# Retention in 64-position chunks with values stacked on state, and all matmuls in program order

## The chip, the cores and the metric

The kernel runs on one core of a Trainium2 chip. A core has a tensor engine (PE), which multiplies a stationary block of weights (loaded by PEld) with a moving block and writes the result to PSUM; a vector engine (DVE), a scalar engine (ACT) and GpSimd (POOL), which work on SBUF (DVE and ACT on PSUM too); and a queue (SP) that issues the DMA transfers between HBM and SBUF. Engines run side by side, each through its own queue in order, and wait for each other by semaphores. The metric is the device time of one execution in microseconds, lower is better.

## The reference, cut to what matters

Two stages. First retention, a linear attention with a decay per head (gamma), over 4 batches, 8 heads, 768 positions and head size 64. Then a gated MLP in which the second half of the hidden layer is normalised and mixed over positions by `w_spatial`.

```python
gamma = 1.0 - 2.0 ** (-5.0 - np.arange(H))
for t in range(S):                                   # S = 768
    state = gamma * state + einsum('bhd,bhe->bhde', k[:, :, t], v[:, :, t])
    y[:, :, t] = scale * einsum('bhd,bhde->bhe', q[:, :, t], state)
x = y.transpose(0, 2, 1, 3).reshape(B, S, 512)
h = np.maximum(x @ w_in, 0.0)                        # 512 -> 1024
u, v = h[..., :512], h[..., 512:]
v_n = (v - mean(v)) / sqrt(var(v) + 1e-6)
v_s = einsum('ts,bsd->btd', w_spatial, v_n) + b_spatial[None, :, None]
out = (u * v_s) @ w_out
```

## The kernel before, in words

**Retention** works chunk by chunk, 128 positions each: 6 chunks a batch, 24 in all, counted by `g`. For one chunk `ret_out` forms the output x of all 8 heads in one PSUM tile: a product of masked scores p and values, plus, from the second chunk of a batch on, a product of the state and the queries. `score` forms the scores of the next chunk, `ret_update` the state after this one. `run(g)` calls the three in this order. All these products have float32 operands, except that from chunk `WHOLE` = 9 on the scores are made from operands that `stack` has split in two float32r parts (`scores_split`). DVE masks the scores of the early chunks (POOL those of the split ones), scales x by the decay of its position into `xf` (L279), and ACT and POOL split `xf` into the float32r parts `xh` and `xl` of the MLP. POOL scales each chunk's values as soon as they are loaded (L211).

**The MLP** takes all its products as three float32r products of high and low parts (`split3`, and L414 in `mlp_out`). `mlp_v` is a block of 128 positions of the second half of the hidden layer (V), `mlp_norm` its normalisation (N). A unit of the gate (I) is the first half of the hidden layer (`mlp_u`, tile u), the spatial product (`mlp_spatial`, tile sp) and the last product (`mlp_out`, tile o) of the unit before it; a batch has 8 units, and O7 closes it. PSUM has three pools: `ps_r` with three buffers for everything in retention, `ps_m` with two for v, u and sp, `ps_o` with three for o.

**The weights** of the MLP come as doubles in 12 blocks. L loads a block into `raw` (three buffers), C splits it (`split_double`): ACT and DVE pick the bits apart (L146 to L152, tiles `da` and `df`), DVE or POOL form the low part. W loads and splits a block of the spatial weights (tile `wst`).

**The order** of the parts is written as four strings of words: START (retention of batch 0 and of the first chunks of batch 1, half of the weights, V and N of batch 0), FIRST (the gate of batch 0, the other weights, the rest of retention and V, N of batch 1), REST (the gate of a batch with retention, V and N of the next), LAST (the last gate). Q loads queries and keys, T keys and values, R runs retention of a chunk. The strings give a scheduler its priorities: loads are held to the program's order on SP, all else, matmuls too, may be moved within an engine's queue by the scheduler's own estimate of times.

Of the kernel before, what the change touches and what calls it, by code (L numbers as in the profile page):

```python
# [9 lines left out]
F32 = mybir.dt.float32  # L10
# [12 lines left out]
WHOLE = 9  # L23
# [7 lines left out]
START = (  # L31
# [3 lines left out]
)  # L35
FIRST = (
    "C7 L10 I0 L11 W01 W11 W21 C8 I1 W31 C9 I2 W51 T12 C10 W41 R9 T11 I3 C11 I4 Q11 R10 "
    "Q12 I5 I6 Q13 R11 V0 I7 V1 N0 V3 V2 N1 N2 T13 N3 V5 V4 N4 N5 O7"
)
REST = (  # L40
    "R0 Q2 T2 R1 I0 I1 Q3 T3 I2 R2 Q4 T5 I3 I4 R3 T4 Q5 I5 R4 Q6 T6 I6 Q7 T7 V0 I7 R5 V1 "
# [5 lines left out]
# Order in which the blocks of the weights in double precision are split, and how many of the  # L47
# residues are formed on the vector engine.
# [7 lines left out]
def tile_retention_gmlp(  # L56
    ctx: ExitStack,
    tc: tile.TileContext,
    qk: bass.AP,
    qT: bass.AP,  # L60
    kT: bass.AP,
    kv: bass.AP,
# [8 lines left out]
    cdecay: bass.AP,  # L71
# [5 lines left out]
    NG = kv.shape[0]  # L77
    NC = NG // B
    H, D = kv.shape[3], kv.shape[4]
    NP = H // 2  # L80
# [16 lines left out]
    mask_t = wpool.tile([P, P], F32, name="mask_t")  # L97
    vd_t = wpool.tile([P, H], F32, name="vd_t")
    qd_t = wpool.tile([P, NP, P], F32, name="qd_t")
    cd_t = wpool.tile([P, NP], F32, name="cd_t")  # L100
# [11 lines left out]
    wout_l = wpool.tile([P, KT, DM], F32R, name="wout_l")  # L112

# [25 lines left out]
    def split_double(i):  # L139
# [3 lines left out]
        a = mpool.tile([P, DM], F32, tag="stage", name=f"da{i}")  # L143
# [19 lines left out]
    query = {}  # L163
    keys = {}
    kvs = {}
    stacked = {}
    scores = {}
    state = {}
    xhalf = {}

    def load_query(g):
        if g >= NG:
            return
        if g < WHOLE:
            t = rpool.tile([P, 2, NP, P], F32, tag="qk", name=f"qk{g}", bufs=3)
            load(t, qk[g])
            query[g] = [t[ROWS[h % 2], 0, h // 2] for h in range(H)]
            keys[g] = t[:, 1]
        else:
            kt = rpool.tile([P, NP, P], F32, tag="qk", name=f"k{g}", bufs=3)  # L180
            qt = rpool.tile([P, H, P], F32, tag="qk", name=f"q{g}", bufs=3)
            load(kt, kT[g - WHOLE])
            load(qt, qT[g - WHOLE])
            query[g] = [qt[ROWS[h % 2], h] for h in range(H)]
            keys[g] = kt
            stack(g, kt, qt)

    def load_value(g):
        if g >= NG:
            return  # L190
        kvs[g] = rpool.tile([P, 2, H, D], F32, tag="kv", name=f"kv{g}")
        load(kvs[g], kv[g])
        scale_v(g)

    def stack(g, kt, qt):
        k2 = mpool.tile([P, H, P], F32R, tag="raw", name=f"k2_{g}", bufs=3)
        q2 = [
            mpool.tile([P, NP, 2, P], F32R, tag="raw", name=f"q2_{g}_{i}", bufs=3)
            for i in range(2)
        ]  # L200
        for r in range(2):
            nc.scalar.copy(k2[ROWS[r], r::2], kt[ROWS[r]])
            residue(nc.vector, k2[ROWS[1 - r], r::2], kt[ROWS[r]], k2[ROWS[r], r::2])
        for i in range(2):
            qi = qt[:, NP * i : NP * i + NP]
            nc.scalar.copy(q2[i][:, :, 0], qi)  # L206
            residue(nc.gpsimd, q2[i][:, :, 1], qi, q2[i][:, :, 0])
        stacked[g] = (k2, q2)

    def scale_v(g):  # L210
        nc.gpsimd.tensor_tensor(  # L211
            kvs[g][:, 1], kvs[g][:, 1], vd_t[:, :].unsqueeze(2).broadcast_to([P, H, D]), ALU.mult
        )

    def scores_split(g):
        k2, q2 = stacked.pop(g)
        ps = []
        for i in range(2):
            p = rpool.tile([P, NP, P], F32, tag="p", name=f"p{g}_{i}", bufs=3)
            for u in range(2):  # L220
                t = ps_r.tile([P, 2, 2, P], F32, tag="ret", name=f"s{g}_{i}_{u}")
                for w in range(2):
# [317 lines left out]
```

## Time and profile before

| | |
|---|---|
| time, median of 3 runs (lowest to highest) | 451.26 us (450.74 to 451.58) |
| span of the profiled execution | 445.8 us |
| granted PE clock, mean | 0.981 |
| busy: PE / PEld / DVE / ACT / POOL | 429.1 / 352.0 / 234.2 / 159.8 / 217.6 us |
| DMA | 45.23 MB, mean 101 GB/s |

The span is what the profile records of one execution, from its first to its last instruction; the median of the runs is 5.5 us above it. Busy times of PE are those of pipelined matmuls, whose ends are modelled, so that records overlap and what a block costs is read from the start of one block to the start of the next. L numbers are lines of the kernel. A float32 matmul leaves two records in the profile, a float32r matmul one.

### The profile page before, as it was taken

How to read it: one execution, taken by the hardware profiler on the slowest of the kernel's cores; microseconds unless marked ns; L12 is line 12 of the kernel's file. 1: busy time of each engine (PE TensorE's matmuls, PEld its weight loads, DVE VectorE, ACT ScalarE, POOL GpSimd, SP SyncE). 2: the span in 40 equal slices, each digit the busy share in tenths (PEclk: the TensorE clock that was granted, in tenths of full speed). 3: DMA queues.
4: the chain of work that ended last, by engine and by line, in shares of the span. 5: the costliest groups of instructions: out<-in, count | busy, mean ns of one | idle time of the engine just before them, and what ended most of it. 6: DMA issues, size and time to landing. Idle time of an engine off the chain costs nothing.

```text
span 445.8 us, 7214 instructions
## 1 busy us (share of the span) xinstructions
PE 429.1 (96%) x2834; PEld 352.0 (79%) x2834; DVE 234.2 (53%) x397; ACT 159.8 (36%) x319; POOL 217.6 (49%) x228
## 2 busy tenths in 40 slices
PE   4998989989999999999999999999999999999995
PEld 2665657777899877887988877888879778999994
DVE  2899989883863556661423556652413534422122
ACT  2324234543434344641433433652423312411211
POOL 1457874695673627473724747365534522211110
PEclk8899999996999999999999999999999999999999
DMA  7846456434125320530213330342313000100102
GB/s 259 312 129 217 130 192 216 147 132 131 43 101 190 93 73 0 209 123 1 96 71 130 109 118 0 102 160 71 96 71 119 1 0 2 71 1 0 72 0 71
DMA packets 16881, 45.23 MB, mean 101 GB/s; under 512 B 2128, under 2 KB 4048, under 8 KB 16848
## 3 DMA queue, kind: packets, MB, share of 16 engines
q1 hardware_dynamic: 16848, 44.77, 29.7%
q8 instruction: 22, 0.36, 0.3%
q14 instruction: 11, 0.09, 0.1%
HBM read 38.48 MB, written 6.29 MB: 100 GB/s over the span
## 4 chain that ended last, share of the span: by engine, by line
PE 77%; DVE 10%; POOL 5%; issue 3%; DMA 3%; SPq 1%; ACT 0%; ACTq 0%; POOLq 0%; DVEq 0%
PE sp L316 22%; PE o L414 14%; PE u L316 14%; PE v L316 11%; PE x L261 6%; PE x L264 5%; PE s L224 3%; PE u L289 2%; DMA kv<-in_kv_dram 1%; DVE p L248 1%; DVE df L149 1%; DMA k<-in_kT_dram 1%; DVE da L151 1%; DVE da L147 1%; DVE da L150 1%
## 5 line engine op out<-in xcount | busy, mean ns | idle before, releaser
L118 POOL TENSOR_TENSOR gl<-t,gh 128x384 fp32r<-128x384 f32 x31 | 32.0, 1032 | 76.2 <-ACT gh L400 72.5
L316 PE MATMUL sp<-wsp_h,vnh 128*128 128x384 f32 x192 | 65.4, 341 | 0.0
L316 PE MATMUL sp<-wsp_l,vnh 128*128 128x384 f32 x192 | 65.0, 339 | 0.0
L316 PE MATMUL sp<-wsp_h,vnl 128*128 128x384 f32 x192 | 64.3, 335 | 0.0
L398 DVE TENSOR_TENSOR t<-sp,bsp_t 128x384 f32<-128x384 f32 (+1 forms) x34 | 17.9, 532 | 76.7 <-PE sp L316 74.3
L261 PE MATMUL x<-p,kv 128*64 128x128 f32 x384 | 45.0, 306 | 6.4 <-POOL kv L211 4.4
L118 POOL TENSOR_TENSOR xl<-xf,xh 128x512 fp32r<-128x512 f32 x24 | 35.0, 1460 | 25.5 <-ACT xh L280 23.3
L118 POOL TENSOR_TENSOR q<-q,q 128x512 fp32r<-128x512 f32 x30 | 41.1, 1380 | 11.9 <-ACT q L206 11.9
L316 PE MATMUL u<-xh,winu_h 128*128 128x384 f32 x128 | 43.9, 343 | 0.0
L261 PEld LDWEIGHTS x<-p,kv 128*64 128x64 f32 x384 | 22.0, 140 | 27.4 <-issue 19.1
L316 PE MATMUL u<-xh,winu_l 128*128 128x384 f32 x128 | 43.5, 340 | 0.0
L316 PE MATMUL u<-xl,winu_h 128*128 128x384 f32 x128 | 43.1, 337 | 0.0
L400 ACT CAST gh<-t 128x384 fp32r<-128x384 f32 (+1 forms) x34 | 16.6, 494 | 68.9 <-DVE t L399 67.8
L316 PE MATMUL v<-winv_h,xh 128*128 128x512 f32 x96 | 39.3, 411 | 0.0
L316 PE MATMUL v<-winv_h,xl 128*128 128x512 f32 x96 | 39.0, 406 | 0.0
L227 DVE TENSOR_TENSOR p<-s,lo 128x256 f32<-128x256 f32 x60 | 23.8, 419 | 28.5 <-ACT lo L226 28.3
L316 PE MATMUL v<-winv_l,xh 128*128 128x512 f32 x96 | 38.7, 404 | 0.0
L211 POOL TENSOR_TENSOR kv<-kv,vd_t 128x512 f32<-128x512 f32 x24 | 26.9, 1120 | 24.0 <-DMA kv<-in_kv_dram 17.9
L228 POOL TENSOR_SCALAR_AFFINE_SELECT p<-p 128x512 f32<-128x512 f32 x30 | 24.2, 808 | 28.8 <-DVE p L227 28.6
L414 PE MATMUL o<-wout_l,gh 128*128 128x512 f32 x96 | 37.5, 394 | 0.0
L316 PEld LDWEIGHTS sp<-wsp_h,vnh 128*128 128x128 f32 x192 | 36.0, 188 | 1.7 <-issue 0.7
L226 ACT COPY lo<-s 128x256 f32<-128x256 f32 x60 | 21.0, 374 | 45.6 <-PE s L224 40.3
(73 smaller groups left out, 878.6 us busy)
## 6 DMA issues: line engine op xcount, KB each, us to landing
kv<-in_kv_dram SPq DMA_DIRECT2D x24, 512.0 KB, 3.5
q<-in_qT_dram SPq DMA_DIRECT2D x15, 512.0 KB, 3.4
out_dram<-ot SPq DMA_DIRECT2D x23, 256.0 KB, 2.0
qk<-in_qk_dram SPq DMA_DIRECT2D x9, 512.0 KB, 5.4
k<-in_kT_dram SPq DMA_DIRECT2D x15, 256.0 KB, 3.6
wst<-in_w_sp_dram SPq DMA_DIRECT2D x12, 192.0 KB, 3.6
raw<-in_w_inv_dram SPq DMA_DIRECT2D x4, 512.0 KB, 6.6
raw<-in_w_inu_dram SPq DMA_DIRECT2D x4, 512.0 KB, 3.8
```

Of the source, the lines that this page charges most:

```text
L118: eng.tensor_tensor(out, whole, high.bitcast(F32), ALU.subtract)
L211: nc.gpsimd.tensor_tensor(kvs[g][:, 1], kvs[g][:, 1], vd_t[:, :].unsqueeze(2).broadcast_to([P, H, D]), ALU.mult)
L224: nc.tensor.matmul(t[:, w], k2[:, NP * i + h], q2[i][:, h], start=True, stop=True)
L226: nc.scalar.copy(low, t[:, :, 1])
L227: nc.vector.tensor_tensor(p[:, 2 * u : 2 * u + 2], t[:, :, 0], low, ALU.add)
L228: nc.gpsimd.affine_select(out=p, in_=p, pattern=[[0, NP], [1, P]], compare_op=ALU.is_ge, fill=0.0, base=0, channel_multiplier=-1,)
L261: nc.tensor.matmul(t[ROWS[r], hp], kvs[g][:, 1, h], ps[h], start=True, stop=(c == 0))
L264: nc.tensor.matmul(t[ROWS[r], hp], state[g][ROWS[r], hp], query[g][2 * hp + r], start=False, stop=True,)
L316: nc.tensor.matmul(ps, l, r, start=(i == 0), stop=(i == 3 * n - 1))
L398: nc.vector.tensor_tensor(t[:, c], pp[:, c], bsp_t[:, tc_], ALU.add)
L400: nc.scalar.copy(gh[:, c], t[:, c])
L414: nc.tensor.matmul(o, l[:, col], r[:, j], start=(j == 0 and n == 0), stop=(j == NJ - 1 and n == 2))
```

## The change

A chunk still has 128 positions, but is worked as two halves of 64 (index `i`). For each pair of heads `hp` and each head `r` of the pair, 64 masked scores and 64 rows of queries lie on top of each other in one tile `pq` of 128 partitions, and 64 values and the 64 rows of the state on top of each other in a tile `vs`. The output of a half is then one product of all 128 rows, without an accumulation. The decay is folded into values and outputs relative to the middle of the batch's sequence, so that the state needs no factor: `ret_update` forms k times v of each half, and the state for the next half is that plus the state before, written by DVE (ACT for the first half of a batch) straight into the rows of `vs`. Scores are float32 for all chunks; the split ones, `stack`, `scale_v` and the third constant are gone. The scores' mask is 64 wide, applied by DVE in four instructions a chunk.

Loads per chunk: two transfers for the queries and one for the keys (Q), two for the values, one for the keys in natural order and one for the table of output decays of this chunk (T); seven where there were two or three. `run` calls update, scores, output in this order. `split_double` takes its tile `da` from the ring of `xf` (two buffers). Every matmul is issued by `mm`, which holds it to the program's order on PE. In the strings, some of the R words of START stand later, and a few T words moved.

```diff
-    "Q0 v m L0 q T0 c Q1 L1 T1 L2 Z R0 Q2 L3 T2 Q3 C0 C1 L4 R1 T3 L5 C2 C3 L6 R2 Q4 T4 V0 "
-    "R3 C4 Q5 T5 V1 N0 L7 R4 V3 W10 Q6 T6 V2 W00 R5 Q7 T7 N1 N2 C5 L8 W40 W20 B W30 R6 Q8 "
-    "T8 V4 N3 R7 Q9 W50 T9 V5 N4 N5 C6 L9 R8 Q10 T10"
+    "Q0 v m L0 T0 Q1 L1 T1 L2 Z R0 Q2 L3 T2 Q3 C0 C1 L4 R1 T3 L5 C2 C3 L6 Q4 T4 R2 V0 "
+    "C4 Q5 T5 R3 V1 N0 L7 R4 V3 W10 Q6 T6 V2 W00 R5 Q7 T7 N1 N2 C5 L8 W40 W20 B W30 Q8 "
+    "T8 R6 V4 N3 Q9 W50 T9 R7 V5 N4 N5 C6 L9 Q10 T10 R8"
...
+    "C7 L10 I0 L11 W01 W11 W21 C8 I1 W31 C9 I2 W51 C10 W41 R9 T11 I3 C11 I4 Q11 R10 "
+    "T12 Q12 I5 I6 Q13 R11 V0 I7 V1 N0 V3 V2 N1 N2 T13 N3 V5 V4 N4 N5 O7"
...
+    def mm(*args, **flags):
+        tc.keep_in_program_order(nc.tensor.matmul(*args, **flags))
...
-        a = mpool.tile([P, DM], F32, tag="stage", name=f"da{i}")
+        a = rpool.tile([P, DM], F32, tag="xf", name=f"da{i}")
...
     def load_query(g):
...
+        m = rpool.tile([P, 2, 2, NP, C], F32, tag="pq", name=f"pq{g}", bufs=3)
+        kt = rpool.tile([P, 2, NP, C], F32, tag="kt", name=f"kt{g}", bufs=2)
+        for r in range(2):
+            load(m[ROWS[1 - r], r], q_in[g, ROWS[1 - r]])
+        load(kt, kT[g])
...
     def load_value(g):
...
+        w = rpool.tile([P, 2, 2, NP, D], F32, tag="vs", name=f"vs{g}", bufs=3)
+        kn = rpool.tile([P, 2, NP, D], F32, tag="kn", name=f"kn{g}", bufs=2)
         for r in range(2):
+            load(w[ROWS[r], r], v_in[g, ROWS[r]])
+        load(kn, k_in[g])
+        qd = rpool.tile([P, NP, P], F32, tag="qd", name=f"qd{g}", bufs=2)
+        load(qd, qdecay[g % NC])
+        values[g], naturals[g], decays[g] = w, kn, qd
+        for r in range(2):
+            vd = vd_t[ROWS[r], g % NC].unsqueeze(3).broadcast_to([D, 2, NP, D])
+            nc.gpsimd.tensor_tensor(w[ROWS[r], r], w[ROWS[r], r], vd, ALU.mult)
+
+    def score(g):
...
+        ts = [ps_r.tile([P, NP, P], F32, tag="ret", name=f"s{g}_{i}") for i in range(2)]
+        for hp in range(NP):
+            for i in range(2):
+                for r in range(2):
+                    col = r if i == 0 else 1 - r
+                    mm(ts[i][ROWS[col], hp, :C], kt[ROWS[1 - r], i, hp],
+                       m[ROWS[1 - r], r, i, hp], start=True, stop=True)
         for i in range(2):
+            for r in range(2):
+                col = ROWS[r if i == 0 else 1 - r]
+                mk = mask_t[col].unsqueeze(1).broadcast_to([C, NP, C])
+                nc.vector.tensor_tensor(m[ROWS[r], r, i], ts[i][col, :, :C], mk, ALU.mult)
+
+    def ret_update(g):
...
+        n = 1 if last else 2
+        ts = [ps_r.tile([P, NP, P], F32, tag="ret", name=f"u{g}_{i}") for i in range(n)]
+        for hp in range(NP):
+            for i in range(n):
+                for r in range(2):
+                    col = 1 - r if i == 0 else r
+                    mm(ts[i][ROWS[col], hp, :D], kn[ROWS[r], i, hp],
+                       w[ROWS[r], r, i, hp], start=True, stop=True)
+        for i in range(n):
+            for r in range(2):
+                u = ts[i][ROWS[1 - r if i == 0 else r], :, :D]
+                dst = w[ROWS[1 - r], r, 1] if i == 0 else values[g + 1][ROWS[1 - r], r, 0]
+                if g % NC == 0 and i == 0:
+                    nc.scalar.copy(dst, u)
+                else:
+                    nc.vector.tensor_tensor(dst, u, w[ROWS[1 - r], r, i], ALU.add)
 
     def ret_out(g):
...
+        t = ps_r.tile([P, NP, 2, C], F32, tag="ret", name=f"x{g}")
+        for i in range(2):
+            for hp in range(NP):
                 for r in range(2):
+                    rows = ROWS[r] if c == 0 and i == 0 else slice(0, P)
+                    mm(t[ROWS[r], hp, i], w[rows, r, i, hp], m[rows, r, i, hp],
+                       start=True, stop=True)
...
     def run(g):
+        ret_update(g)
+        score(g + 1)
         ret_out(g)
-        score(g + 1)
-        ret_update(g)
```

Two places show how the instructions stand. The first is PE's queue around the retention of chunk 15, in the gate of batch 1; s16 are the scores of the next chunk, u15 the update, sp1_1_1 a spatial product. Before, these rows stand there:

```order
L316 MATMUL sp1_1_1_2378<-wsp_h_84,vnl1_1574 128x384
L224 MATMUL s16_1_0_2319<-q2_16_1_2160,k2_16_2158 128x256 x2
L316 MATMUL sp1_1_1_2378<-wsp_h_84,vnh1_1573 128x384
L224 MATMUL s16_1_1_2325<-q2_16_1_2160,k2_16_2158 128x256 x2
L289 MATMUL u15_2332<-kv15_2039 64x64 x8
L316 MATMUL sp1_1_1_2378<-wsp_l_85,vnh1_1573 128x384
```

The scheduler had put the scores and the update between the matmuls of a spatial product. In the same place on PE now (u15_0 and u15_1, s16_0 and s16_1 alternate four times each):

```order
L110 MATMUL u15_0_2525<-vs15_2278,kn15_2279 64x64 x2
L110 MATMUL u15_1_2526<-vs15_2278,kn15_2279 64x64 x2
L110 MATMUL s16_0_2547<-pq16_2402,kt16_2403 64x64 x2
L110 MATMUL s16_1_2548<-pq16_2402,kt16_2403 64x64 x2
...
L110 MATMUL x15_2569<-pq15_2273,vs15_2278 64x64 x16
L110 MATMUL u1_2_1_2606<-xh9_1423,winu_h_80 128x384
```

Update, scores and output stand in one piece, with nothing between them, and the next product of the gate behind them.

The second place is DVE's queue in START, around the split of the weight block with number 5 (tiles da5 and df5); p and pq are masked scores, bst and mv belong to the normalisation. Before, it begins there:

```order
L279 TENSOR_TENSOR xf2_302<-x2_285,qd_t_75 128x512
L150 TENSOR_SCALAR da4_412<-df4_413 128x512
L147 TENSOR_SCALAR da5_606<-da5_606 128x512
L151 SCALAR_TENSOR_TENSOR da4_412<-raw4_206,da4_412 128x512
L118 TENSOR_TENSOR df4_413<-df4_413,winu_h_82 128x512
L148 TENSOR_SCALAR da5_606<-da5_606 128x512
```

Split 5 was mixed into split 4, right behind the output of chunk 2. Now on DVE:

```order
L266 TENSOR_TENSOR xf5_772<-x5_755,qd5_493 128x512
L145 TENSOR_SCALAR da5_796<-da5_796 128x512
L116 TENSOR_TENSOR vnl0_449<-vr0_2_709,vnh0_448 128x512
L146 TENSOR_SCALAR da5_796<-da5_796 128x512
L241 TENSOR_TENSOR vs7_781<-u6_1_837,vs6_687 64x256 x2
L147 SCALAR_TENSOR_TENSOR df5_797<-raw5_343,da5_796 128x512
L148 TENSOR_SCALAR da5_796<-df5_797 128x512
L215 TENSOR_TENSOR pq7_776<-s7_0_858,mask_t_73 64x256 x2
L215 TENSOR_TENSOR pq7_776<-s7_1_859,mask_t_73 64x256 x2
L149 SCALAR_TENSOR_TENSOR da5_796<-raw5_343,da5_796 128x512
L266 TENSOR_TENSOR xf6_899<-x6_880,qd6_692 128x512
L116 TENSOR_TENSOR wsp_l_83<-wst4_0_809,wsp_h_82 128x384
```

The split has moved behind the output of chunk 5, and the low part of spatial block 4 stands after it.

More of the change, by code (lines that the diff above doesn't have):

```diff
@@ L95, in tile_retention_gmlp @@
     ps_o = ctx.enter_context(tc.tile_pool(name="ps_o", bufs=3, space=bass.MemoryType.PSUM))
[L97 to L100, printed above, removed]
+    mask_t = wpool.tile([P, C], F32, name="mask_t")
+    vd_t = wpool.tile([P, NC, 2, NP], F32, name="vd_t")
     bsp_t = wpool.tile([P, S], F32, name="bsp_t")
@@ L161, in split_spatial @@
         residue(pick(c + NC * half < VECTOR_SPATIAL), wsp_l[:, c, cols], st, wsp_h[:, c, cols])
-    query = {}
+    queries = {}
     keys = {}
[L165 to L168, printed above, removed]
+    naturals = {}
+    values = {}
+    decays = {}
     xhalf = {}
@@ L173, in load_query @@
             return
[L174 to L186, printed above, removed]
+        m = rpool.tile([P, 2, 2, NP, C], F32, tag="pq", name=f"pq{g}", bufs=3)
[3 more added lines that the diff above has]
+        load(kt, kT[g])
+        queries[g], keys[g] = m, kt
     def load_value(g):
@@ L254, in ret_out @@
     def ret_out(g):
         b, c = divmod(g, NC)
[L256 to L268 removed]
+        m, w = queries.pop(g), values.pop(g)
```

183 lines of the change are left out of this document (57 added, 126 removed).

## The prediction

> **What bounds the kernel now.** I read the busy time by stretch first, then the chain that ended last, then the timelines of PE, DVE and SP. Columns of the first view: stretch, length, busy time of PE, PEld, DVE, ACT and POOL with their instructions, granted clock, DMA share, GB/s.
>
> ```profile
> 0.00:16.00 16.00, 10.38 (x75) 6.65 (x75) 6.53 (x13) 4.54 (x6) 4.37 (x9) 0.79 0.84 307
> 16.00:43.00 27.00, 24.24 (x225) 15.48 (x222) 26.96 (x46) 8.46 (x14) 15.68 (x15) 1.00 0.55 182
> 43.00:86.50 43.50, 41.68 (x322) 30.26 (x321) 40.05 (x60) 16.35 (x30) 29.70 (x30) 0.96 0.53 176
> 117.00:441.00 324.00, 324.00 (x2011) 278.14 (x2009) 139.46 (x248) 117.04 (x241) 146.92 (x159) 1.00 0.21 72
> ```
>
> There are two kernels in one. From 16 to 86.5 us DVE is busy 67.0 of 70.5 us and sets the pace. From 117 to 441 us PE never rests. Cheaper matmuls pay in the second part only; DVE work and waits pay in the first.
>
> The chain that ended last gives the price of each block of the MLP (start, length, engine, tile, line, records):
>
> ```profile
> 374.25 8.16 PE v L316 x36
> 406.64 3.12 PE sp L316 x18
> 409.76 2.08 PE o L414 x9
> 411.85 2.10 PE u L316 x12
> 441.07 0.64 ACTq L536
> ```
>
> A unit of the gate is 2.10 + 3.12 + 2.08 = 7.30 us, and 32 of them are 233.6. A V block is 8.16 / 3 = 2.72; batches 1 to 3 need 18, or 49.0. These 282.6 us are not changed. After the last product (about 440.9) 4.9 us remain to the span's end at 445.8.
>
> **Retention on PE, before.** The PE timeline around chunk 15 (start, length, operands, records), and a state update:
>
> ```profile
> 302.56 0.69 PE L289 MATMUL u<-kv 128*64 128x64 f32 x16
> 303.18 0.73 PE L414 MATMUL o<-wout_h,gl 128*128 128x512 f32 x2
> ```
> ```profile
> 331.16 0.43 PE L261 MATMUL x<-p,kv 128*64 128x128 f32 x2
> 331.52 0.43 PE L264 MATMUL x<-q,st 64*64 64x128 f32 x4
> ...
> 333.73 0.43 PE L264 MATMUL x<-q,st 64*64 64x128 f32 x4
> 334.09 0.73 PE L224 MATMUL s<-q,k 128*128 128x256 f32 x4
> 334.66 0.34 PE L316 MATMUL u<-xh,winu_h 128*128 128x384 f32 x1
> ```
>
> The output takes 334.09 - 331.16 = 2.93 us in eight steps of 0.37, changing array shape at each; half the scores take 334.66 - 334.09 = 0.57, so 1.14; the update 0.62. A chunk costs 4.69. A float32 matmul leaves two records. The update's sixteen are eight matmuls of 64 columns, two halves of the array at once. Its 0.62 holds about 0.15 of draining, so a two-record pair costs 0.46 / 4 = 0.12.
>
> **Retention on PE, after.** The update and the scores are sixteen 64x64x64 matmuls each, four to a step on four quarters of the array; the output is sixteen of the update's old shape, eight pairs. Nothing in the trace uses four quarters at once. Nearest is the row above, two halves by columns, and this one, two by rows, whose 144 records of 302 ns overlap into 14.3 us:
>
> ```profile
> L244 PE MATMUL s<-qk 64*128 64x128 f32 x144 | 14.3, 302 | 0.1
> ```
>
> If both ways combine, sixteen matmuls cost 0.46 and a drain; if only pairs run together, 0.93. I take 0.46, since each direction alone overlaps; 0.93 stays as the upper end, and I see no reason for less than 0.46. The Trainium skill, "TensorE: Matmul & The Clock Gate", Part 3, says that tiles which differ in rows and in columns run concurrently, and shows it for sixteen; by it, as by my choice, the sum stays as below. No run here shows the four.
>
> But pinning adds a wait. Five score, update and output tiles per chunk share three PSUM buffers (ps_r). On PE the order is update, scores of the next chunk, output. The second score tile needs the buffer of the first update tile, so PE stands until DVE has added that tile to the state. The output needs the second one. DVE's price (two additions of 256 elements from PSUM) and its reaction to PE are:
>
> ```profile
> 88.06 0.74 DVE L227 TENSOR_TENSOR p<-s,lo 128x256 f32<-128x256 f32 x2
> 334.21 0.69 DVE L279 TENSOR_TENSOR xf<-x,qd_t 128x512 f32<-128x512 f32 x1 [3.81 <-PE x L264]
> ```
>
> (PE's last record ended at 333.73 + 0.43 = 334.16, DVE began 0.05 later.) So, from the update's start: update done 0.69; first tile added 0.05 + 0.74, 1.48; scores go on at 1.55; second tile added by 2.16 (0.74 more, less an overlap that I put at 0.06); output starts 2.25, lasts 8 x 0.12 + 0.15 = 1.09; with 0.1 for entering, **3.43 us**. About 1.1 of it is waiting that other matmuls could fill if they were free to. Chunks 9 to 23, which lie in the PE-bound part: ten at 3.43; chunks 12 and 18 (no old state; ACT takes one tile) 3.3 each, and 0.5 each where the next chunk follows at once and waits for buffers; chunks 11 and 17 (half an update) 2.6; chunk 23, without scores, 2.1. Sum 34.3 + 7.6 + 5.2 + 2.1 = 49.2. Before, by the rows above, the same chunks cost 63.7 (13 outputs of 2.93, two of 1.0 without state, 14 scores of 1.14, 12 updates of 0.62), plus the drains where they are mixed into other blocks. ACT and POOL lose the copies and residues of the split scores; they wait there anyway, so I cost that at nothing. The scaling of the values becomes two POOL instructions of 64 rows for one; it is hidden while POOL has 30 of 43 us busy.
>
> **START, after.** Now PE may not begin the gate before R8 is done, and R8 is DVE's affair. DVE groups up to 86.5 us, where before has just ended the gate's first sp (busy us, mean ns):
>
> ```profile
> L248 DVE TENSOR_TENSOR p<-s,mask_t 128x512 f32<-128x512 f32 x18 | 12.0, 678 | 0.8 <-PE s L244 0.8
> L151 DVE SCALAR_TENSOR_TENSOR da<-raw,da 128x512 f32<-128x512 uint32 x9 | 8.8, 983 | 0.1
> L149 DVE SCALAR_TENSOR_TENSOR df<-raw,da 128x512 int32<-128x512 int32 x9 | 7.5, 839 | 0.1
> L147 DVE TENSOR_SCALAR da<-da 128x512 f32<-128x512 f32 x9 | 6.1, 680 | 7.3 <-ACT da L146 7.3
> L279 DVE TENSOR_TENSOR xf<-x,qd_t 128x512 f32<-128x512 f32 x8 | 5.4, 679 | 0.4 <-PE x L261 0.4
> L150 DVE TENSOR_SCALAR da<-df 128x512 int32<-128x512 int32 x9 | 5.3, 589 | 0.0
> L148 DVE TENSOR_SCALAR da<-da 128x512 int32<-128x512 int32 x9 | 5.2, 579 | 0.1
> L298 DVE TENSOR_TENSOR sm<-u,st 128x256 f32<-128x256 f32 x5 | 2.1, 414 | 0.0
> L118 DVE TENSOR_TENSOR k<-k,k 64x512 fp32r<-64x512 f32 x2 | 1.4, 688 | 1.0 <-ACT k L202 1.0
> L295 DVE TENSOR_TENSOR st<-u,cd_t 128x256 f32<-128x256 f32 x2 | 0.8, 410 | 0.0
> ```
>
> DVE has done 6.53 + 26.96 + 40.05 = 73.5 us there. Up to xf of chunk 8, after loses masks 12.0, states 2.9, keys 1.4 and two of nine splits, 2 x 32.9 / 9 = 7.3; it gains 40 masks and 30 state additions of 0.37 (14.8 + 11.1) and one xf (0.7): **76.5 us**. To it come the times in which DVE must stand. I walked its new queue with these durations:
>
> ```profile
> 0.79 0.38 SPq L115 DMA_DIRECT2D qk<-in_qk_dram  x1
> 1.23 0.42 SPq L115 DMA_DIRECT2D vd_t<-in_vdecay_dram  x1
> ...
> 63.16 0.38 SPq L115 DMA_DIRECT2D raw<-in_w_out_dram  x1
> ...
> 71.64 0.43 SPq L115 DMA_DIRECT2D qk<-in_qk_dram  x1
> ```
> ```profile
> 3.11 6.62 DMA kv<-in_kv_dram
> 9.87 1.12 POOL kv L211
> ```
> ```profile
> wst<-in_w_sp_dram SPq DMA_DIRECT2D x12, 192.0 KB, 3.6
> ```
>
> First, 12.0 by 16 us: SP issues a transfer every 0.45, so the values are issued near 4, land near 8, POOL scales twice 1.12, the first update starts at 10.4, and DVE's queue holds chunk 0 and 1 ahead of the first split. Second, 2 around 41, for V0, which waits in PE's queue for the last low part of winv with R3 behind it. Third, 3 at 58: W00's load stands on SP behind chunk 6's decay table, whose buffer comes free with xf of chunk 4. Fourth, 1.5 at 64, POOL's rs behind a scaling. Fifth, 4.3 at 76: splits now share a ring of two with xf, so split 5 comes after xf of chunk 5 and ends at 76 where before sent raw8 at 63.16; raw8, W40, W20 and chunk 8's queries (71.64 before) all wait on SP for it, and a block lands 3.6 later. With 1.2 of small ones the holes are 24.0. Another 2 for hand-overs of 0.05 at some forty places. xf of chunk 8 ends at 102.5; PE's output of chunk 8 ends 2.5 before (five DVE instructions lie between), at **100.0**.
>
> Then the gate starts with DVE in arrears: winu's third block low part, 0.3; the first sp's tile waits behind two splits, 1.3; winu's fourth, 1.8: 3.4. In R10 the queries of chunk 11 stand on SP behind the output stores of I4: 1.7.
>
> **Sum:** 100.0 + 3.4 + 282.6 + 49.2 + 1.7 + 4.9 = 441.8 us of span, against 445.8. The runs' median is 451.26, 5.5 above the profiled span, so I forecast **447 us**, 1% faster: some 15 us won in the PE-bound part, more than two thirds of them given back in START.
>
> **Rivals.** (1) START runs longer, and the kernel is slower. The place is split 5 and SP's queue: everything PE does after s of chunk 8 waits for it, and nothing else can move up. It decides once the gate starts over 4.9 us later than 100.0 (445.8 + 0.9 - 441.8); with 10 us more, 457. For it: the holes I found are those I looked for. Against it: the first 16 us and DVE's sum are firm. (2) Four quarters do not run at once: 0.47 more per update, 0.15 more where the scores become the later one: 0.6 x 13, 8 us, 455. (3) The clock. The stretch 0 to 16 had 0.79 granted, and at half clock a pair of output steps took
>
> ```profile
> 102.90 0.62 PE x L261 x4
> ```
>
> instead of 0.37. Pinned PE stands longer in START. If its six V blocks ran at half clock, 6 x 2.7 = 16 us more, half of it beside DVE: 455. The Trainium skill, same page, Part 1, puts the clock at half after an idle window of about 3.4 us; the 0.79 behind the first wait agrees, and by it V0 and V5 at least would be hit. I leave them out, since DVE is later than PE at both. (4) Gains and losses cancel within 0.9 us. (5) The change does more: DVE's holes of 58 and 76 us close, 440.
>
> **How the numbers follow.** Forecast and (5), faster: 0.42 and 0.11. (4): 0.10. (1): 0.20. (2): 0.10. (3): 0.07. So faster 0.53, same 0.10, slower 0.37, where 0.2% (0.9 us) is what a measurement here can tell from nothing. Both signs hold much: the forecast's own range is 441 to 450; the range given, 434 to 462, takes in (2), (3), most of (1), and (5) with still fewer holes.
>
> **What would show it.** Right: a steady chunk of about 3.4 us from the update's first matmul to the gate's next one, with PE waiting for DVE's state additions once or twice in it; sixteen u or s records stepping by 58 ns in fours; the gate's first u near 100 us; DVE idle near 58 and 76 us behind wst loads; then PE full but for R blocks. Wrong: chunks over 4 us, the first u before 95 or after 104, or waits inside the V and gate blocks after 130 us, of which the sum has none.

## The result, and the profile after

The changed kernel takes **483.2 us** (median of 4 runs, 481.6 to 484.8) against 451.0 beside it: 1.073 times as long, interval 1.069 to 1.077. The forecast was 447, range 434 to 462. The profiled execution has a span of 479.8 us for 445.8. Times of the runs further down are medians of all their executions; one of the four of e14_ring_q and one of the four of e17_combo_pinned was a slow one, over 1.5% above the fastest, and without it their medians are 474.9 and 459.8 us.

The page of the changed kernel: busy time of each engine, and the 40 slices of the span for PE and for its granted clock.

```profile
PE 395.0 (82%) x3786; PEld 351.7 (73%) x3786; DVE 231.5 (48%) x445; ACT 112.0 (23%) x207; POOL 164.6 (34%) x176
...
PE   3536683655799789997999999969999999999996
...
PEclk9656596777799979998999999998999999999999
```

The redesign did what it says to the matmuls: PE is busy 34 us less than the 429.1 of before. But it stands for 85 us where it stood for 17, and most of that in the first ten slices. To date the end of the start-up I take the gate's first sp on PE. Timeline of before, then of after:

```profile
81.16 0.44 PE L316 MATMUL sp<-wsp_h,vnh 128*128 128x384 f32 x1
```
```profile
124.20 0.69 PE L110 MATMUL sp<-wsp_h,vnh 128*128 128x384 f32 x1 [3.59 <-ACT ur L340]
```

Cut there, these are the stretches of before and then of after (busy us of PE, PEld, DVE, ACT, POOL, then the clock, the DMA share, GB/s):

```profile
0.00:81.16 81.16, 70.97 (x586) 47.83 (x587) 68.23 (x110) 27.73 (x47) 45.84 (x49) 0.94 0.61 209
81.16:445.80 364.64, 358.18 (x2252) 304.19 (x2248) 165.95 (x289) 132.04 (x273) 171.73 (x180) 0.99 0.23 78
```
```profile
0.00:124.20 124.20, 67.22 (x986) 54.24 (x986) 84.98 (x156) 28.91 (x51) 54.61 (x58) 0.72 0.62 173
124.20:479.80 355.60, 327.80 (x2800) 297.50 (x2800) 146.48 (x290) 83.13 (x157) 109.95 (x119) 0.97 0.24 73
```

The start-up is 43.0 us longer, the rest 9.0 shorter: together the 34 us of the spans. The two start-ups don't hold quite the same: before, eight chunks' outputs (xf) lie in it, now nine, since the pin puts chunk 8 ahead of the gate. In the start-up no engine is full: DVE has 16.8 us more work before that point, and 39.2 us of idle time for 12.9. In the rest PE has 30.4 us less to do and waits 27.8 us for 6.5, so that two thirds of that gain are gone as well.

What PE waits for until 124.2, the five largest (us in total, times, the longest):

```profile
PE s L110 <- DMA kt<-in_kT_dram: 13.0, 5, 7.7
PE s L110 <- DVE mv L310: 8.4, 2, 6.7
PE u L110 <- POOL vs L191: 7.6, 5, 5.4
PE x L110 <- DVE vs L241: 6.9, 4, 4.0
PE u L110 <- DMA kn<-in_k_dram: 5.6, 1, 5.6
```

Loads, POOL's scaling and DVE's additions come last in turn, from chunk to chunk (where "mv" is named, what frees the score tile is the first update tile's two additions, which stand in DVE's queue just ahead of it). A steady late chunk on PE:

```profile
367.75 0.69 PE L110 MATMUL u<-vs,kn 64*64 64x64 f32 x32
368.26 0.28 PE L110 MATMUL s<-pq,kt 64*64 64x64 f32 x4
369.50 0.68 PE L110 MATMUL s<-pq,kt 64*64 64x64 f32 x28 [0.95 <-DVE vs L241]
370.41 1.15 PE L110 MATMUL x<-pq,vs 128*64 128x64 f32 x32 [0.22 <-DVE vs L241]
371.49 0.44 PE L110 MATMUL u<-xh,winu_h 128*128 128x384 f32 x1
```

From 367.75 to 371.49 it takes 3.74 us (3.43 forecast): two scores start, and the other fourteen wait for the buffer of the first update tile, as the prediction said (a matmul leaves two records here). And chunk 10, whose query loads come late:

```profile
163.72 0.69 PE L110 MATMUL u<-vs,kn 64*64 64x64 f32 x32
169.42 1.24 PE L110 MATMUL s<-pq,kt 64*64 64x64 f32 x32 [5.00 <-DMA kt<-in_kT_dram]
170.59 1.97 PE L110 MATMUL x<-pq,vs 128*64 128x64 f32 x32
172.49 0.69 PE L110 MATMUL u<-xh,winu_h 128*128 128x384 f32 x1
```

8.8 us for 5.1 forecast, its scores and output at half speed (granted clock 0.50 from 169.4 to 172.4).

### The profile page after: what moved, and what is told of

It reads as the page before. It is cut to its first block, busy times and chain, and to the rows that moved or that the text cites. A ratio compares the mean times of both kernels' runs of the same rounds, so it can differ in the third digit from the quotient of the medians.

```text
span 479.8 us, 9219 instructions
## 1 busy us (share of the span) xinstructions
PE 395.0 (82%) x3786; PEld 351.7 (73%) x3786; DVE 231.5 (48%) x445; ACT 112.0 (23%) x207; POOL 164.6 (34%) x176
## 5 line engine op out<-in xcount | busy, mean ns | idle before, releaser
L191 POOL TENSOR_TENSOR vs<-vs,vd_t 64x512 f32<-64x512 f32 x48 | 52.4, 1091 | 90.7 <-DMA vs<-in_v_dram 78.4
L116 POOL TENSOR_TENSOR gl<-t,gh 128x384 fp32r<-128x384 f32 x31 | 31.6, 1019 | 109.0 <-ACT gh L366 108.6
L110 PE MATMUL s<-pq,kt 64*64 64x64 f32 x768 | 25.5, 258 | 45.0 <-DMA kt<-in_kT_dram 21.2
L110 PEld LDWEIGHTS s<-pq,kt 64*64 64x64 f32 x768 | 21.0, 165 | 48.2 <-issue 17.3
L215 DVE TENSOR_TENSOR pq<-s,mask_t 64x256 f32<-64x256 f32 x96 | 40.5, 422 | 15.3 <-PE s L110 7.6
L110 PE MATMUL x<-pq,vs 128*64 128x64 f32 (+1 forms) x768 | 37.7, 267 | 10.1 <-DVE vs L241 10.0
L110 PE MATMUL u<-xh,winu_h 128*128 128x384 f32 x128 | 45.3, 354 | 0.0
L116 POOL TENSOR_TENSOR xl<-xf,xh 128x512 fp32r<-128x512 f32 x24 | 31.2, 1299 | 37.9 <-ACT xh L269 37.1
L241 DVE TENSOR_TENSOR vs<-u,vs 64x256 f32<-64x256 f32 x80 | 33.8, 422 | 21.5 <-PE u L110 14.6
L110 PEld LDWEIGHTS x<-pq,vs 128*64 128x64 f32 (+1 forms) x768 | 33.8, 176 | 13.2 <-issue 6.5
L110 PE MATMUL o<-wout_h,gl 128*128 128x512 f32 x96 | 38.0, 395 | 0.0
```

The source lines that it names most:

```text
L110: tc.keep_in_program_order(nc.tensor.matmul(*args, **flags))
L116: eng.tensor_tensor(out, whole, high.bitcast(F32), ALU.subtract)
L191: nc.gpsimd.tensor_tensor(w[ROWS[r], r], w[ROWS[r], r], vd, ALU.mult)
L215: nc.vector.tensor_tensor(m[ROWS[r], r, i], ts[i][col, :, :C], mk, ALU.mult)
L241: nc.vector.tensor_tensor(dst, u, w[ROWS[1 - r], r, i], ALU.add)
```

## The experiments

All are edits of the changed kernel. "First sp" and "rest" are the two stretches above, from each profile. Ratios are to the kernel before beside them, with their intervals.

| run | us | ratio | first sp | rest |
|---|---|---|---|---|
| before | 451.0 | | 81.2 | 364.6 |
| changed kernel | 483.2 | 1.073 (1.069 to 1.077) | 124.2 | 355.6 |
| e1_free: nothing pinned | 478.4 | 1.066 (1.061 to 1.071) | 132.9 | 346.9 |
| e2_ret_free: retention free | 494.1 | 1.099 (1.094 to 1.104) | 124.5 | 368.4 |
| e2_mlp_free: all but retention free | 465.1 | 1.034 (1.029 to 1.039) | 117.7 | 342.8 |
| e3_swap: output ahead of scores | 472.2 | 1.050 (1.046 to 1.054) | 114.2 | 356.8 |
| e5_warm: dummy matmuls | 491.9 | 1.094 (1.089 to 1.099) | 129.4 | 360.5 |
| e7_ring: splits' own ring | 479.8 | 1.067 (1.062 to 1.073) | 123.0 | 352.4 |
| e8_qdlate: tables later | 484.2 | 1.077 (1.070 to 1.083) | 117.1 | 362.4 |
| e9_first: two splits first | 484.9 | 1.078 (1.074 to 1.083) | 124.2 | 359.4 |
| e6_late: chunks 6 to 8 later | 491.9 | 1.096 (1.088 to 1.103) | 94.8 | 393.5 |
| e10_nosplit: no splits on DVE | 469.4 | 1.045 (1.037 to 1.052) | 118.0 | 353.2 |
| e12_free_swap: mlp_free + swap | 457.9 | 1.017 (1.011 to 1.023) | 111.4 | 344.3 |
| e11_combo: that + ring + late | 443.7 | 0.988 (0.982 to 0.994) | 86.8 | 352.4 |
| e14_ring_q: ring + tables | 476.0 | 1.054 (1.047 to 1.061) | 119.5 | 353.6 |
| e15_nosplit_q: nosplit + tables | 459.5 | 1.021 (1.017 to 1.026) | 105.8 | 350.8 |
| e16_combo_q: e11 + tables | 438.7 | 0.975 (0.971 to 0.980) | 87.0 | 349.1 |
| e17_combo_pinned: e11, all pinned | 461.5 | 1.022 (1.014 to 1.029) | 92.1 | 362.6 |
| e18_three: ring + tables + swap | 465.0 | 1.038 (1.032 to 1.043) | 117.5 | 344.6 |
| e19_all_pinned: e16, all pinned | 460.9 | 1.027 (1.022 to 1.032) | 95.8 | 361.3 |

### The pin, or the redesign

```diff
     def mm(*args, **flags):
-        tc.keep_in_program_order(nc.tensor.matmul(*args, **flags))
+        nc.tensor.matmul(*args, **flags)
```

> The changed kernel with no matmul pinned; transfers stay in program order. Theory A (the pin is the loss: each chunk's matmuls stand in one queue behind their own loads, additions and buffers, and whatever is ready behind them stands too): the redesign alone wins. The pinned trace has 2.2 us of matmuls per chunk (0.52 + 0.6 + 1.08) against 4.7 before; with the waits filled the time should be 400 to 430 us, the gate should start well before 116 us, and waits inside the gate's blocks should nearly vanish. Theory B (the redesign itself is the loss: four small masks and four small additions on DVE per chunk, 221 transfers on one queue): no more than 2% from 483 us. Theory C (the loss is the clock, at half speed after PE's waits): the matmuls that ran at half speed in the pinned trace (some 20 us of excess) recover, and not much more, 460 to 470 us.

478.4 us: theory A fell. The late part does become 8.7 us shorter, but the start-up 8.7 longer; both profiled spans are 479.8. The time is theory B's. Of the two causes that B names, DVE's work is not it, since DVE is idle for 46 us in that start-up; the one queue of transfers this run can't tell. Which matmuls should be free was the next question.

The same edit for the matmuls of `score`, `ret_update` and `ret_out` alone, and for those of `split3` and `mlp_out` alone:

> The changed kernel with the retention matmuls free and those of the gate, its values and the output pinned in their order. Theory A says that it is the retention matmuls that wait, and that freeing them is enough: within 10 us of the kernel with nothing pinned. If instead the big matmuls must be able to move up into the waits, it stays over 460 us. Theory B: 483 us within 2%.

> The changed kernel with the retention matmuls pinned among themselves and all others free. Theory A: the big matmuls fill the 1.5 us hole of each steady chunk (15 chunks, some 20 us) and the waits at the batch boundaries, but in the start-up they have little that is ready, since the chain of chunks with its loads still runs in order: 445 to 460 us. If the start-up's length is also set by the big matmuls standing behind the chunks, it comes down to the kernel with nothing pinned. Theory B: 483 us within 2%.

Freeing the retention makes it worse, 494.1: in the order that came out, the scores wait longer for their keys (21.2 us in the changed kernel).

```profile
PE s L113 <- DMA kt<-in_kT_dram: 34.5, 7, 11.7
```

Freeing the big matmuls brings 18.1 us, a little less than expected. Between the profiled spans it is 12.8 in the late part, where they fill the chunks' holes, and 6.5 in the start-up. So one half of the pin costs and the other helps, and with the better choice the redesign is still 3.4% slower than before: the rest is 22 us shorter, the start-up 36 longer.

### The order within a chunk

```diff
         ret_update(g)
-        score(g + 1)
         ret_out(g)
+        score(g + 1)
```

> Everything pinned as in the changed kernel, but each chunk's output is issued ahead of the next chunk's scores: update, output, scores. Theory A: the output no longer stands behind the score load of the next chunk (21.2 us of waits on kt in all), nor behind the second update tile's buffer. Worked out: update 0.52, two additions 0.07 + 0.87, second half of the output 0.54 later, scores on free buffers 0.6, 2.9 us in a steady chunk for 3.74, 13 us over the 15 late chunks, and some 12 us of the start-up: about 455 us (445 to 465). Theory D (the start-up is as long as DVE's work and the weight loads make it, whatever the order on PE): the gate still starts after 112 us, 468 to 474 us. Theory C: 475 us or more.

472.2, a time of theory D, though the gate's first u came at 108.6 where D had it after 112 (first sp 10.0 us earlier). A steady chunk takes 3.3 us for 3.74 (2.9 forecast): now the output waits for the state. But the rest did not get shorter (356.8 for 355.6): chunks 9 to 23 take 55.4 us there for 64.5, and the gate, which starts earlier, waits 7.4 us for parts of winu that are not split yet. The chain of a steady chunk, in order of time:

```profile
371.86 0.64 PE u L110 x32
...
372.52 0.43 DVE vs L241
...
372.98 0.43 DVE vs L241
...
373.45 0.68 PE x L110 x14
```

### Single holds in the start-up

The dummy matmuls go to a PSUM tile that nothing reads, ahead of the steps named:

```diff
+    before = {"u": {1: 20, 6: 8}, "s": {1: 10, 2: 6, 4: 14, 7: 28, 8: 24}, "x": {5: 14}}
     def run(g):
+        stir(before["u"].get(g, 0))
         ret_update(g)
+        stir(before["s"].get(g, 0))
         score(g + 1)
...
```

> The changed kernel, pinned, with dummy 128x512 bf16 matmuls (0.2 us each) issued into PE's longest waits of the start-up: 20 and 8 ahead of the updates of chunks 1 and 6, 10, 6, 14, 28 and 24 ahead of the scores issued by chunks 1, 2, 4, 7 and 8, 14 ahead of the output of chunk 5, 14 ahead of the gate's first sp. They compute nothing that is used. Theory C (the clock): the blocks that ran at half speed behind waits (values 0.43 for 0.23 us, sp 0.32 for 0.17, output 1.90 for 1.08, scores 1.17 for 0.6), some 20 us of excess until the first sp has ended, run at full speed, and the gate's first sp starts 8 to 15 us earlier: 468 to 475 us. Theory E (the start-up's length is set by DVE, SP's queue and transfers, and PE only waits for them): the granted clock rises to over 0.95, but the first sp moves by less than 4 us plus what the first sp itself gains (2.8): 478 to 484 us.

The mean granted clock rose from 0.906 to 0.939, not to what was expected, and the time by 8.7 us, more than either theory allowed; the first sp came 5.2 later. The dummies themselves take PE time where waits had moved, so this doesn't price the clock, and it neither shows theory C nor rules it out: a higher mean clock came with a longer start-up, but with 138 matmuls more in it.

```diff
-        a = rpool.tile([P, DM], F32, tag="xf", name=f"da{i}")
+        a = rpool.tile([P, DM], F32, tag="da", name=f"da{i}")
...
-        xf = rpool.tile([P, NP, P], F32, tag="xf", name=f"xf{g}")
+        xf = rpool.tile([P, NP, P], F32, tag="xf", name=f"xf{g}", bufs=1)
```

> The changed kernel with the splits' scratch tile on a ring of its own (two buffers; the retention's output tile has one then, for which there is room). The prediction's step: the shared ring makes split 5 late and so the loads behind it, some 4 us. Theory E with this as the cause: raw8 is issued by 80 us where it was at 88.8, and the time falls to 476 to 480 us. If the ring is not what holds the splits: 482 to 485 us.

```diff
-        qd = rpool.tile([P, NP, P], F32, tag="qd", name=f"qd{g}", bufs=2)
-        load(qd, qdecay[g % NC])
+        for n in [g - 1] * (g > 0) + [g] * (g == NG - 1):
+            qd = rpool.tile([P, NP, P], F32, tag="qd", name=f"qd{n}", bufs=2)
+            load(qd, qdecay[n % NC])
```

> The changed kernel with each chunk's decay table loaded one chunk later in SP's order (with the next chunk's values), so that its wait for the output of two chunks before no longer holds back the weights' and score loads behind it. Theory E with SP's queue as the cause: SP's waits for xf (33.0 us in all) go, PE's waits for kt (21.2 us in all) fall to under 10, also at the batch boundaries, and the time is 465 to 474 us. If those loads are held up by the splits anyway, over 479 us.

```diff
-    "Q0 v m L0 T0 Q1 L1 T1 L2 Z R0 Q2 L3 T2 Q3 C0 C1 L4 R1 ...
+    "Q0 v m L0 T0 C0 Q1 L1 T1 L2 C1 Z R0 Q2 L3 T2 Q3 L4 R1 ...
```

> The changed kernel with the first two splits of the weights written ahead of the first chunk in the program, so that DVE splits block 0 in its first idle time (7 to 17 us) rather than behind chunks 0 and 1. Theory E with the late start of DVE as the cause: block 0 is split by 16 us where it was 24.5, the raw loads on SP follow 8 us earlier, the first sp starts 6 to 9 us earlier, 474 to 478 us. If the start-up is a chain of chunks and loads that does not hang on the splits: 481 to 485 us.

479.8, 484.2 and 484.9. The first lies in the range of the ring's theory, but by luck: raw8 is issued at 90.0 us and not by 80 (88.8 in the changed kernel), the gate's first u stays (115.8 for 115.9), the first sp comes 1.2 us earlier, and the rest of the gain lies behind it. In e8_qdlate the first sp comes 7.1 us earlier and the rest is 6.8 longer. In e9_first block 0 is split by 14.5 us and the next raw load goes out at 16.4 for 24.0, as expected, but by the load at 59.2 (59.8 before) the lead is gone. What SP's queue waits for until 124.2 shows why. After, then with the own ring, then with the tables later, then without the splits on DVE (below):

```profile
SPq L113 <- DVE da L149: 42.8, 8, 10.3
SPq L113 <- DVE da L145: 12.2, 2, 8.9
SPq L113 <- DVE xf L266: 7.4, 2, 4.2
```
```profile
SPq L113 <- DVE xf L266: 50.2, 7, 10.1
```
```profile
SPq L113 <- DVE da L149: 53.1, 7, 11.2
```
```profile
SPq L113 <- DVE xf L256: 39.4, 6, 9.4
```

SP stands for 39 to 62 us in each: for the splits (the raw buffers come free) or for the retention's outputs (the table's buffer comes free). Take one away, and it stands for the other.

### Work taken out of the start-up

```diff
-    ... B W30 Q8 T8 R6 V4 N3 Q9 W50 T9 R7 V5 N4 N5 C6 L9 Q10 T10 R8"
+    ... B W30 V4 N3 W50 V5 N4 N5 C6 L9"
-    "C7 L10 I0 L11 W01 W11 W21 C8 I1 W31 C9 I2 W51 C10 W41 R9 T11 I3 ...
+    "C7 L10 I0 Q8 T8 R6 L11 W01 W11 W21 C8 I1 Q9 T9 R7 W31 C9 I2 Q10 T10 R8 W51 C10 W41 I3 R9 T11 ...
```

> The changed kernel, pinned, with chunks 6, 7 and 8 and their loads taken out of the start-up and put between the first items of the gate (one behind each of the items 0, 1 and 2); the first batch needs only chunks 0 to 5. In the pinned trace these three lie between 78 and 116 us, with waits of 7.7 and 6.7 us in them. Theory F (the start-up is a ring of queues, in which each chunk costs some 12 us because SP, DVE and PE wait for each other in turn, so fewer chunks make it shorter): the first sp starts 18 to 28 us earlier than at 124.2, the chunks cost 4 to 8 us each among the items, 462 to 472 us. Theory G (the start-up ends when the weights are split and loaded, whatever the chunks): the first sp moves by less than 8 us, over 480 us.

The first sp comes 29.4 us earlier, some 10 us for each chunk moved: theory F for the start-up. But the total is 8.7 us worse, where F had it better by 11 or more: the rest is 37.9 us longer, since the pinned gate, started earlier, now waits for weights and for the chunks among its items. PE's waits in that run from 94 to 170 us:

```profile
PE s L110 <- DVE vs L241: 6.0, 3, 4.2
PE u L110 <- ACT winu_h L150: 5.2, 1, 5.2
PE o L110 <- POOL wout_l L152: 4.0, 1, 4.0
```

```diff
-        nc.scalar.activation(a, top.bitcast(F32), AF.Abs)
...
-        nc.vector.scalar_tensor_tensor(a, low.bitcast(U32), 2.0**-52, a, ALU.mult, ALU.mult)
-        nc.scalar.copy(hi, f)
-        residue(pick(i < VECTOR_BLOCKS), f, f, hi)
-        nc.gpsimd.tensor_tensor(lo, f, a, ALU.add)
+        nc.scalar.copy(hi, top.bitcast(F32))
+        nc.gpsimd.tensor_tensor(lo, top.bitcast(F32), hi.bitcast(F32), ALU.subtract)
```

> The changed kernel without DVE's part of the splitting of the twelve weight blocks: the high part is a copy of each number's upper word by ACT, the low part one subtraction on POOL, so the weights are wrong and DVE does 3.5 us less per block (nine blocks in the start-up, 31 us). Loads and matmuls are the same. Theory G (the splits, and the loads that wait for their buffers, set the start-up): a chunk in the start-up comes down from 12 us to below 9 and the first sp starts at 85 to 100 us, 445 to 458 us. Theory H (the chain of chunks itself: load, scaling, update, addition, scores, mask, output, one chunk after the other): the first sp stays after 112 us, 470 us or more. Theory F lies between, 100 to 112 us.

Its first sp is at 118.0, as theory H had it, the total (469.4) just under H's range. The stretch up to there:

```profile
0.00:118.04 118.04, 66.33 (x986) 53.36 (x987) 52.78 (x110) 24.52 (x43) 53.15 (x58) 0.73 0.67 184
```

DVE lost 32 of its 85 us, and the start-up 6: DVE's amount of work alone doesn't bound it.

The next runs put edits together that stand above.

> Retention pinned among itself with the output ahead of the next scores, all other matmuls free. The two gains found one by one were 18.1 us (others free) and 11.0 us (output first). If they are gains on different waits they add up, 452 to 456 us; if free matmuls already fill the hole that the other order closes, 461 to 466 us.

> As the run with free gate matmuls and output ahead of scores, and also the splits' own ring and chunks 6 to 8 out of the start-up. Theory F: these act on the start-up, the others on the late chunks, so it comes to the time of the kernel before or below, 432 to 450 us. Theory G: no more than 5 us below the run without them.

457.9, between the two expectations, and 443.7. The order and the free matmuls together bring 25.3 of the 29.1 us that they bring apart. With the ring and the three chunks moved too, the kernel is 1.2% faster than before. What made e6_late slow is gone, and for the larger part not because the big matmuls are free: with the same edits and all matmuls pinned (e17_combo_pinned, below) the time is 461.5 for e6_late's 491.9, and PE no longer waits for weights between 94 and 170 us. How the 14.2 us between e12 and e11 divide between the ring and the chunks no run shows.

### Two and three holds together

> The changed kernel, pinned, with both the splits' own ring and the decay tables loaded one chunk later. Alone they gave -3.4 and +1.0 us. Theory J (two holds in one queue, each hiding the other): SP's waits for splits and for outputs in the start-up, 50 us or more in each of the runs with one of them, fall below 30 us together, the first sp starts before 110 us, 460 to 470 us. Theory H (the chain of chunks is as long as that): within 4 us of the better of the two, 476 to 484 us.

> The changed kernel, pinned, without DVE's part of the splits (as in the run without them: the weights are wrong) and with the decay tables one chunk later, so that neither holds SP. Alone they gave -13.8 and +1.0 us. Theory J: a chunk in the start-up takes 6 to 9 us where it took 12, the first sp starts at 80 to 100 us, 440 to 458 us. Theory H: first sp after 110 us, 464 to 470 us.

Both brought more than their parts: -7.2 us (-8.3 by 474.9) for -3.4 and +1.0, which the spread of the first pair's runs (471 to 479) hardly tells from the sum; -23.7 for -13.8 and +1.0, which is clear. So in the second pair the holds do cover each other. But neither reached theory J's times (460 to 470, 440 to 458), and the first sp came to 119.5 and 105.8, not before 110 and 100. With the first pair SP's waits for splits are down to 16.5 us and those for xf are gone, but it stands 24.8 us for PE's outputs instead, and PE stands for the update's buffers, whose additions wait in DVE's queue:

```profile
SPq L113 <- PE x L110: 24.8, 4, 6.6
SPq L113 <- DVE da L149: 16.5, 3, 8.1
```
```profile
PE s L110 <- DVE mv L312: 17.6, 4, 6.5
```

> The run that was faster than the kernel before (free gate matmuls, output ahead of scores, splits' own ring, chunks 6 to 8 out of the start-up; 443.7 us) with the decay tables one chunk later as well. There SP waited 41.7 us for outputs until 135 us. Theory J: another 4 to 10 us, 433 to 440 us. Theory H: within 3 us of 443.7.

438.7 us, a time of theory J: **2.5% faster than before**, the best kernel of the study. SP's 41.7 us of waits for xf are gone, but the first sp stays (87.0 for 86.8); the gain is in the rest.

> The run of 443.7 us with every matmul pinned again (output ahead of scores, splits' own ring, chunks 6 to 8 out of the start-up). If the pin costs the same whatever the start-up (18.1 us between the changed kernel and that with free gate matmuls, 14.4 with the output first): 456 to 464 us. If the pin's cost lies in the waits of the start-up, and moving chunks 6 to 8 among the items of a pinned gate makes it wait for weights, as in the pinned run with only that change (491.9 us): 470 us or more.

> The changed kernel, pinned, with the splits' own ring, the decay tables one chunk later and the output ahead of the scores; all nine chunks stay in the start-up. Alone the output first gave -11.0 us, the other two together -7.2. Theory J (three holds that cover each other): more than their sum, the first sp before 106 us, 450 to 461 us. Theory H (the chain of chunks): their sum or less, 465 to 474 us.

> The kernel of 438.7 us (output ahead of scores, splits' own ring, chunks 6 to 8 out of the start-up, tables one chunk later, gate matmuls free) with every matmul pinned again. Without the later tables the same step cost 17.8 us. If the pin's cost is the 1 us hole of each late chunk and the weight waits of the first items, which the tables do not touch: 454 to 460 us. If later tables also mend the waits of the pinned items: below 452 us.

With all three holds gone the gain is 18.2 us, the plain sum: theory H's statement, if for a time at the lower edge of its range. Of the spans' 17.7 us, 11.0 lie in the rest (344.6 for 355.6); the first sp, at 117.5, moved by 6.7. Pinning the big matmuls costs much the same everywhere: 18.1 us in the changed kernel, 14.4 with the output first, 17.8 (e17 over e11; 16.1 by 459.8) and 22.3 (e19 over e16) with the start-up mended, most of it in the rest. e18 and e19 differ in the three chunks' place alone: with them among the gate's items the first sp comes 21.7 us earlier, the rest is 16.7 us longer, and the time falls by 4.1 us.

**What is shown and what is open.** Shown: two causes. The pin on the big matmuls costs 14 to 22 us, most of it after the start-up. And each chunk in front of the gate puts off its start by 7 to 10 us (21.7 us for three between e18 and e19, 29.4 between the changed kernel and e6); neither the pin, nor the splits on DVE, nor one load's place makes the start-up long by itself. Every run with nine chunks there has its first sp at 106 to 133 us, every one with six at 87 to 96. An earlier first sp is not time won, though: with all matmuls pinned, moving the chunks cost 8.7 us by itself and won 4.1 with the three holds gone, since the work moved with them and the gate waited in its turn. Open is how the 7 to 10 us of a chunk divide between loads, POOL's scaling and DVE's queue, and what the start-up's low clock (0.72 for 0.94) has in it.

## Why the prediction was wrong

By its own sum, forecast and measured (span):

| term | forecast | measured |
|---|---|---|
| gate's first u on PE | 100.0 | 115.9 |
| stalls as the gate begins | 3.4 | 7.3 |
| chunks 9 to 23, with chunk 10's stall | 50.9 | 64.5 |
| the MLP's fixed time | 282.6 | 287.8 |
| tail | 4.9 | 4.3 |
| sum | 441.8 | 479.8 |

**START is the step that failed first**, and as rival (1) put it: it decides from 104.9 on, and the gate began at 115.9. That is 15.9 of the 38.0 us by which the sum is off; the late chunks are 13.6, the gate's beginning and the fixed time 9.1. Of the 15.9, DVE's work is 3.0 and its idle time 12.9. The work to chunk 8's xf was 79.5 us for 76.5, since the small operations take 0.42 and not 0.37 (70 of them, 3.5 us):

```profile
L215 DVE TENSOR_TENSOR pq<-s,mask_t 64x256 f32<-64x256 f32 x96 | 40.5, 422 | 15.3 <-PE s L110 7.6
...
L241 DVE TENSOR_TENSOR vs<-u,vs 64x256 f32<-64x256 f32 x80 | 33.8, 422 | 21.5 <-PE u L110 14.6
```

DVE's idle time was 38.9 for 24 + 2. The named holes are there: 12.3 us in the first 16, spatial blocks behind the tables and behind split 5 (3.9 at 72 and 4.6 at 94, forecast 58 and 76). But 4.1 at 34 (a raw block late), 2.5 at 106 and others came on top, and every later hole was later than the walk had it. The walk took the holes one by one and let everything else run on time. The runs show a ring instead, in which SP, DVE, POOL and PE wait for each other. Taking split 5's ring away, which the prediction priced at 4.3 us of START, gave 3.4 us, but the nearness is luck: raw8 went out no earlier (90.0 for 88.8), as SP then stood for the tables, and the gate's first u stayed (115.8 for 115.9).

**The late chunks.** The steady chunk was 3.74 for 3.43: PE stands 0.95 + 0.22 us in it for DVE's four additions of 0.43. Seven of them make 2.2 us; entering and leaving the chunk costs the blocks around it some 0.2 each, part of the 5.2 in the fixed time. The bulk is in three places where loads are late: chunk 10 (8.8 for 5.1) and the two batch boundaries, where two chunks follow each other (10.7 and 11.0 for 7.2 each). The forecast had one stall of 1.7 us here. (Its 63.7 us for the same chunks before add up to 63.5.) The Trainium skill, "Perfetto Trace Analysis", Optimization Strategy, says that the same gap repeating on the engine that should be full can mean too little SBUF or PSUM for the next tile; the 0.95 us in every chunk is of that kind, since the score tile waits for an update tile's buffer.

**Four quarters, rival (2).** Right as forecast: the update's sixteen matmuls take 368.26 - 367.75 = 0.51 us (0.46 and a drain; 0.93 if only pairs ran together).

**The clock, rival (3).** Half speed did appear, in the values of START (here within one block: starts 0.43, then 0.23 us apart), in outputs, scores and the first sp:

```profile
88.44 0.63 PE L110 MATMUL v<-winv_h,xh 128*128 128x512 f32 x1
...
89.47 0.40 PE L110 MATMUL v<-winv_h,xh 128*128 128x512 f32 x1
```

That it is the cause is not shown: e5_warm raised the clock, and the time with it, by matmuls that take time themselves. What half speed costs by itself stays open.

**The signs to look for.** The first u after 104 us was named as a sign of being wrong; the steady chunk stayed under the 4 us named, and DVE was idle behind wst loads as said, but at 72 and 94 us. The waits after 130 us are in the chunks, not in the gate's own blocks. The chance of 0.20 for rival (1) was too low, since the sum rested on a list of holes that nothing bounded from above.

## What to carry to other kernels

When a redesign cuts work on the bound engine but adds transfers, small instructions and buffers per step, look at the stretch where no engine is full, and don't price its waits one at a time: behind each stands another in the same queue, and removing one may show nothing. Count how many steps stand in front of the point that starts the bound engine: moving three chunks behind it brought that point forward by 22 to 29 us, more than any single repair. But look at the total too, since what starts earlier may wait for something else: alone the move made the kernel slower, and it paid only together with the repairs. Leave the long work that is ready free to move into the short work's waits: pinning it cost some 20 us of 440 here, while pinning the short chain itself helped.

## What the runs showed of the hardware

A DVE operation on 64 partitions costs what one on 128 does: 422 ns for 64x256 (above), 419 for 128x256 before. The same on POOL, 1120 ns for 128x512 before and 1091 for 64x512 after. Groups of before, then of after:

```profile
L227 DVE TENSOR_TENSOR p<-s,lo 128x256 f32<-128x256 f32 x60 | 23.8, 419 | 28.5 <-ACT lo L226 28.3
...
L211 POOL TENSOR_TENSOR kv<-kv,vd_t 128x512 f32<-128x512 f32 x24 | 26.9, 1120 | 24.0 <-DMA kv<-in_kv_dram 17.9
```
```profile
L191 POOL TENSOR_TENSOR vs<-vs,vd_t 64x512 f32<-64x512 f32 x48 | 52.4, 1091 | 90.7 <-DMA vs<-in_v_dram 78.4
```

Halving the partitions thus about doubled POOL's scaling time (52.4 us for 26.9), and PE's start-up waited 7.6 us for it, where it had waited 4.4 before. And PE's speed goes here with the length of the wait ahead:

```profile
63.84 1.15 PE L110 MATMUL x<-pq,vs 128*64 128x64 f32 x32 [0.31 <-DVE vs L241]
...
75.75 1.98 PE L110 MATMUL x<-pq,vs 128*64 128x64 f32 x32 [4.01 <-DVE vs L241]
```

After a wait of 4.0 us the output's sixteen matmuls took 1.98 us at a granted clock of 0.50, after short waits (0.31, and 1.69 just ahead of it) 1.15 at 1.00. The Trainium skill, "TensorE: Matmul & The Clock Gate", Part 1, puts the clock at half after an idle window of about 3.4 us; the rows agree.
